# A new order for nearly all steps of a fused RWKV-7 and exact-GELU kernel

## The chip, the cores and the metric

The kernel runs on one core of one Trainium2 chip. The metric is the device time of one execution in microseconds (us); where a number of runs is given, it is their median. TensorE does the matrix products, VectorE and ScalarE the elementwise work, GpSimd fills constants and inverts small triangular blocks, and SyncE (SP) issues nearly all of the transfers. Each engine runs its own list of instructions in order, and waits on semaphores for the others.

## The reference

Two blocks follow each other. The first is the RWKV-7 recurrence over 768 steps for 4 batches and 8 heads of 40 columns; the second is a feed-forward block with the exact GELU. Cut to what is computed:

```python
# r, k, v, w, a, b: (4, 8, 768, 40) float32; state: (4, 8, 40, 40), zero at first
for t in range(S):
    y[:, :, t] = einsum('bhd,bhde->bhe', rt, state)
    Sa = einsum('bhde,bhe->bhd', state, at)
    state = state * wt[:, :, None, :] - einsum('bhd,bhe->bhde', Sa, bt)
    state = state + einsum('bhd,bhe->bhde', vt, kt)
x = y.transpose(0, 2, 1, 3).reshape(3072, 320)
h = x @ w_in                                    # w_in: 320 x 2048
g = 0.5 * h * (1.0 + erf(h * sqrt(0.5)))
return g @ w_out                                # w_out: 2048 x 320
```

`w_in` and `w_out` arrive as 64-bit floats. The kernel receives them as pairs of 32-bit words and makes 32-bit floats of them on the chip.

## The kernel before

**Chunks.** The sequence is cut into 12 chunks of 64 steps of time. Inside a chunk the recurrence is written as matrix products: cumulated decays, products of the scaled rows (`N`, `A`, `RV`, `QY`), the inverse of a unit triangular matrix of 64 x 64 for each head, and the state carried to the next chunk. The feed-forward block for the 256 rows of a chunk follows once its `y` is there. Chunks overlap: while the products of one chunk run, the inverse of the next one is under way and the feed-forward block of the one before fills TensorE.

**Steps.** Every piece of work is a *step*: a generator function whose name is a kind and a chunk, `N3` or `ph5`. Each time that a step is advanced, it emits the instructions up to its next `yield`. The kinds that matter here are these.

- `w`, `a`, `b`, `k`, `v`, `r` load a chunk's inputs (helper `load`, line 228, a DMA on SP's queue); `wi`, `wl` and `wo` load the words of the two weight matrices.
- `logs` (line 520) takes the logarithm of the decays in `w_tile`; `sums` forms their running sums on TensorE with the triangular mask `cum_m`; `sc` and `sk` scale the rows with them.
- `ta`, `tb`, `tk`, `tv`, `tr` are transposes on TensorE, through the helper `mm` of line 160, as most of the recurrence's products are.
- `N` is the product whose triangular part has to be inverted. It is written to memory by DMA. `nb` brings its 32 x 32 blocks back, with one block to a partition, to the tile `Nb`; `inv` inverts them on GpSimd, with 31 pairs of instructions for a chunk (lines 825 and 827), and stores the result. `corner` and `joined` bring it into place and multiply the blocks together. Chunk 0 has a way of its own, on TensorE: `sq`, `cornerd`, `joinedd`.
- `A`, `RV`, `av`, `X`, `sa`, `tn`, `yy`, `qk`, `QY`, `y` and `state` finish the chunk's recurrence.
- `ph` is the first feed-forward product, in a plain form for chunks 0 to 2 (line 1197) and in a form with fewer multiplications after that (lines 1222 and 1229). `pc`, `pd` and `pg` combine its parts and apply GELU on ScalarE and VectorE (lines 1258 to 1274); `po` is the second product (lines 1300 and 1316) and stores the output.
- `ci` and `co` turn the words of `w_in` and `w_out` into floats. VectorE and ScalarE share that work (lines 473 to 494).
- `consts`, `zeros`, `pads`, `gaps` and `tails` fill constant parts of tiles, nearly all on GpSimd; `consts` makes `cum_m` (line 353), `zeros2` clears columns of `VR`.
- `warm` and `begin` issue matmuls whose results nobody reads. `begin6` first has VectorE set a part of `w_in_sb` to 1 (line 1394), and then issues six of them.

TensorE takes its results in four tiles `duo0` to `duo3`, of two banks of PSUM each. A step that needs one takes the tile whose number stands behind its token.

**The order.** No scheduler orders the steps. A text of 1,554 tokens, `ORDER`, names at each place which step is advanced next, and after a colon which `duo` tile (and for conversions, which scratch tile) it takes:

```python
    ctx.enter_context(tc.manual_schedule(engines={mybir.EngineType.PE, mybir.EngineType.SP,
                                                 mybir.EngineType.DVE, mybir.EngineType.Pool,
                                                 mybir.EngineType.Activation}))
    going = {}
    for token in ORDER.split():
        queue[0] = nc.scalar if token[0] == "*" else nc.sync
        name, *at = token.strip("*").split(":")
        places[:] = [int(x) for x in at]
        if name not in going:
            kind = name.rstrip("0123456789")
            going[name] = steps[kind](int(name[len(kind):]))
        next(going[name], None)
```

So the list of instructions of each of the five engines, SP's transfers among them, is what this text lays down. A *pass* below is one weight load and one matmul as the hardware runs them; a product in 32-bit floats with one `matmul` call takes two passes. TensorE has 14,128 passes in an execution.

Of the kernel before, what the change touches and what calls it, by code (L numbers as in the profile page):

```python
# [34 lines left out]
sq1:1 sq1 placed0 av0:3 cornerd0 av0 tr1:0 ci9 wl0 shifts0 v1 tk1:2 cornerd0:1 wi0 ci4:1 placed2 zeros2 w2 tv1:3 cornerd0 consts0 joinedd0:1  # L35
r2 tr1 warm5:0 tv1 wo0 logs2 joinedd0 placed1 ci2:2 ci5 inv1 ci2 inv1 placed3 joinedd0 ci2 av0:3 av0 wi0 sums2:0 wi0 sa0:1
sa0 ci4 tk1 sa0:3 sums2:2 sa0 co1:0 a2 QY0:1:3 ci4 qk0 state0 sums2 y0 ta2:2 A1:1 tn1:3 co0:2 sums2 ci3:1 nb1 wi1
ci3 wi1 A1 co1 zeros8 r2 RV1:0 b2 co0 ta2 zeros6 wq3 tn1 y0:1 ci3 RV1 tr2:3 wi1 sc2 y0:2 tr2 y0
y0 inv1 yy1:3 yy1 av1:0:2 yy1 inv1 wi1 k2 co0 ci6:1 zeros5 ci7:2 tb2:1 inv3 wi1 co1 tb2 ci6 wo2 v2 ph0:3
ph0 sk2 ci7 inv1 ci6 zeros7 N2:1 ph0 X1 N2 ph0:1 wi1 ph0 co3:0 co3 ft1 ci7 X1 ci8:1 corner1:2 corner1:3 wo4  # L40
ci8 ph0 tk2:0 ft1 tv2:1 inv2 ft1 a3 co3 co2:2 a3 corner1 X1 co4:0 joined1:3 tk2 N2 A2:2 co2 ci8 co4 tv2
co2 joined1 ph0:0 A2 ph0 N2 ta3 wo6 ph0 joined1 co4 nb2 wo15 co7:1 co6:2 sa1:1:2 sa1 co6 co5:0 co7 wq3 w3
co6 bp3 RV2:3 ph0:0 sa1 ph0 wt3:2 QY1:1:2 w3 qk1 co7 RV2 co5 co5 tables1 wo9 bp3 po0:3 y1 po0 po0 state1
inv2 wt3 tn2:1 inv2 wo10 ph0 co11:1 k3 nb2 y1 y1 av2:0:2 logs3 wo8 tn2 vp3 y1 yy2:1 co11 kp3 wt3 kp3
y1 co11 inv2 po0 vp3 yy2 wt3 yy2 wo14 co8:0 co9:1 X2 tb3 co9 co8 ph1:1 ta3 tk3:2 X2 X2 ph1 sums3:0
sums3 co14:2 b3 co9 co14 r3 ph1 co8 wo13 co15:1 co10:0 N3:2 wo12 ph1:0 ph1 vp3 co15 co14 a4 co15 inv2 vp3
co13:2 N3 inv2 N3 co12:1 co10 N3 sc3 ft2 ph1 co12 co10 ft2 nb3 co13 r3 co12 ph1:1 ph1 tv3 A3:0 po1:2
nb3 co13 tails1 r3 po1 corner2:0 inv4 po0 po0 ft2 A3 corner2:0 po0 corner2 a4 ph1 po0 wq4 ta4 joined2:0 joined2 po0
r3 tr3 ph1:1 po0 joined2 sa2:3:0 wq4 wt4:1 sa2 ph1 wt4 bp4 sa2 QY2:3:0 wt4 qk2 ph1 bp4 sk3 po1 y2 state2
inv3 v3 vp4 RV3:1 RV3 po1 inv3 w4 w4 vp4 vp4 po0 vp4 tv4 wt4 y2 kp4 kp4 tn3:3 av3:0:1 tn3 yy3:3  # L50
tb4 yy3 y2 y2 po1 yy3 X3 a5 ta4 tk4:2 wq5 po0 N4:3 inv3 po1 N4 y2 po1 wq5 N4 wt5:0 ph2:3
X3 ws0 N4 inv3 inv3 ph2 wt5 ph2 ph2:0 ph2 ph2 r4 r4 ph2:3 ww0:1 ww0 nb4 nb4 inv4 wt5 ft3 logs4
ft3 inv4 ft3 corner3:2 ph2 ws1 ww0 ph2 corner3:0 corner3 po1 ws3 joined3:3 r4 a5 r4 po1 ph2:0 po1 vp5 vp5 ws2
# [24 lines left out]
kp9 ta9 kp9 yy8 wq10 po6 po6:2 wq10 po6 yy8 N9:3 po6 po6 po6 X8 X8 N9 po6:2 tk9:2 y7 N9 N9
po6 logs8 wt10:0 inv8 b8 tx7 tx7 po6 po6 po6:3 sums8:1 po6 inv10 wt10 nb9 tx7 nb9 wt10 X8 A9:2 A9 ft8
# [1363 lines left out]
```

## Time and profile before

| | before |
|---|---|
| median of 3 runs | 657.48 us (653.74 to 660.06) |
| profiled execution, its own time | 653.45 us |
| its span | 651.7 us |
| TensorE matmuls busy | 630.6 us, 97% |
| VectorE busy | 483.7 us, 74% |
| ScalarE busy | 273.5 us, 42% |
| GpSimd busy | 385.8 us, 59% |
| data moved by DMA | 80.78 MB, mean 124 GB/s |

The span runs from the first to the last instruction of the core; the execution's own time also holds what lies around it, 1.75 us here. TensorE's row is the one to read first: what it is not busy is all that an order of the same instructions can win back, unless the passes themselves run differently. In the tables of waits, the name behind the arrow is the instruction that ended an idle time; "issue" stands where the profile shows none.

### The profile page before, as it was taken

The numbers are of one execution on the slowest core, as the hardware profiler recorded it, in microseconds if no ns is written. First come the engines' busy times: TensorE is split into PE (matmuls) and PEld (weight loads), VectorE is DVE, ScalarE is ACT, GpSimd is POOL, SyncE is SP. The second block draws the span as 40 slices with busy tenths as digits, with TensorE's granted clock in tenths as the row PEclk, the third lists the DMA queues.
The fourth block names the chain that finished last, engine by engine and source line by source line (L and its number), as shares of the span: only waits on it lengthen the run. The fifth ranks groups of instructions, "written<-read, shape, count | busy, mean of one in ns | idle before, by whom it ended". The sixth has DMA issues, their size and how long they took to land.

```text
span 651.7 us, 31510 instructions
## 1 busy us (share of the span) xinstructions
PE 630.6 (97%) x14128; PEld 570.3 (88%) x14128; DVE 483.7 (74%) x643; ACT 273.5 (42%) x326; POOL 385.8 (59%) x797
## 2 busy tenths in 40 slices
PE   8998999999999999999999999999999899999997
PEld 4887778787888999999989988999999899999987
DVE  0797999996878997876967987886894884834442
ACT  2566465442434333524534345444433445135130
POOL 5058836845857866847857856868824877811000
PEclk9999999999999999999999999999999999999999
DMA  9989988679676867876786767697677866340100
GB/s 133 159 167 190 177 144 193 147 146 163 122 149 111 154 126 127 151 128 121 137 149 107 139 123 138 119 167 134 118 118 144 133 116 109 60 71 5 31 12 22
DMA packets 299112, 80.78 MB, mean 124 GB/s; under 512 B 287688, under 2 KB 292560, under 8 KB 298976
## 3 DMA queue, kind: packets, MB, share of 16 engines
q1 hardware_dynamic: 297872, 76.23, 65.1%
q0 software_dynamic: 864, 2.36, 2.2%
q8 instruction: 111, 1.82, 1.2%
q14 instruction: 25, 0.20, 0.1%
q10 hardware_dynamic: 240, 0.16, 0.1%
HBM read 65.40 MB, written 11.01 MB: 117 GB/s over the span
## 4 chain that ended last, share of the span: by engine, by line
PE 74%; DVE 7%; DMA 7%; SPq 6%; issue 3%; ACT 1%; POOL 1%; DVEq 0%; POOLq 0%; ACTq 0%
PE duo L160 22%; PE duo L1316 19%; PE duo L1222 15%; PE duo L1197 8%; SPq L228 6%; PE duo L1300 6%; PE duo L1229 4%; DMA inv<-rT 1%; DMA Tt<-inv 1%; DMA rows<-in_k_dram 1%; DMA rows<-N 1%; DMA rT<-in_k_dram 1%; DMA inv<-W 1%; DVE conv L493 1%; DMA rows<-in_b_dram 1%
## 5 line engine op out<-in xcount | busy, mean ns | idle before, releaser
L825 POOL TENSOR_TENSOR tmp<-W,Nb 128x56 f32<-128x56 f32 (+22 forms) x155 | 75.9, 490 | 56.6 <-DMA Nb<-N 45.0
L825 POOL TENSOR_TENSOR tmp<-rT,Nb 128x56 f32<-128x56 f32 (+22 forms) x155 | 78.6, 507 | 37.0 <-DMA Nb<-N 25.1
L1316 PE MATMUL duo<-w_out_sb,gt 128*128 128x160 f32 x640 | 93.2, 302 | 2.6 <-ACT gt L1274 1.2
L1316 PEld LDWEIGHTS duo<-w_out_sb,gt 128*128 128x128 f32 x640 | 87.7, 190 | 5.8 <-ACT gt L1274 1.4
L827 POOL TENSOR_TENSOR W<-W,tmp 128x56 f32<-128x56 f32 (+22 forms) x155 | 77.2, 498 | 12.2
L827 POOL TENSOR_TENSOR rT<-rT,tmp 128x56 f32<-128x56 f32 (+22 forms) x155 | 66.6, 430 | 12.1
L1222 PE MATMUL duo<-xt,w_in_sb 64*128 64x128 f32 x864 | 61.5, 275 | 0.0
L1266 DVE TENSOR_TENSOR gt<-gt,duo 128x1024 f32<-128x1024 f32 x27 | 32.7, 1213 | 34.6 <-ACT gt L1260 18.6
L1260 ACT COPY gt<-duo 128x1024 f32<-128x1024 f32 x27 | 27.3, 1012 | 73.7 <-PE duo L1222 46.3
L1229 PE MATMUL duo<-xt,w_in_sb 64*128 64x128 f32 x576 | 56.2, 272 | 0.0
L1197 PE MATMUL duo<-xt,w_in_sb 64*128 64x256 f32 x480 | 54.8, 381 | 1.0 <-DVE N L698 0.9
L1222 PEld LDWEIGHTS duo<-xt,w_in_sb 64*128 64x128 f32 x864 | 54.2, 188 | 1.7 <-DVE spare L698 0.5
L1197 PEld LDWEIGHTS duo<-xt,w_in_sb 64*128 64x128 f32 x480 | 45.5, 187 | 7.4 <-DVE N L698 1.2
L1316 PE MATMUL duo<-extra,conv 128*128 128x160 f32 x320 | 46.7, 302 | 1.2 <-issue 1.0
L1316 PEld LDWEIGHTS duo<-extra,conv 128*128 128x128 f32 x320 | 44.0, 190 | 2.3 <-issue 1.3
L1229 PEld LDWEIGHTS duo<-xt,w_in_sb 64*128 64x128 f32 x576 | 44.1, 188 | 0.0
L1272 ACT ACTIVATE gt<-gt 128x1024 f32<-128x1024 f32 x27 | 28.3, 1057 | 31.3 <-DVE gt L1266 31.3
L627 POOL TENSOR_TENSOR rows<-rows,w_tile 128x640 f32<-128x640 f32 x9 | 15.3, 1699 | 39.6 <-ACT w_tile L543 26.2
L1300 PE MATMUL duo<-w_out_sb,gt 128*128 128x320 f32 x128 | 36.9, 440 | 0.0
L1300 PEld LDWEIGHTS duo<-w_out_sb,gt 128*128 128x128 f32 x128 | 23.6, 190 | 9.4
L1320 DVE TENSOR_TENSOR os<-os,duo 128x160 f32<-128x160 f32 x40 | 12.7, 318 | 25.2 <-PE duo L1316 22.4
L968 ACT COPY SM<-duo 128x832 f32<-128x832 f32 (+1 forms) x22 | 17.4, 829 | 24.6 <-PE duo L160 24.6
(257 smaller groups left out, 1415.4 us busy)
## 6 DMA issues: line engine op xcount, KB each, us to landing
Nb<-N SPq DMA_DIRECT2D x18, 256.0 KB
VR<-in_v_dram SPq DMA_DIRECT2D x24, 160.0 KB
out_dram<-os SPq DMA_DIRECT2D x45, 80.0 KB
rows<-in_b_dram SPq DMA_DIRECT2D x22, 160.0 KB
rows<-in_k_dram SPq DMA_DIRECT2D x22, 160.0 KB
w_out_sb<-in_moe_w_out_dram SPq DMA_DIRECT2D x5, 640.0 KB
w_tile<-in_w_dram SPq DMA_DIRECT2D x36, 80.0 KB
Tt<-inv SPq DMA_DIRECT2D x44, 64.0 KB
```

Source lines behind the costliest of these rows:

```text
L160: nc.tensor.matmul(o, lhsT, rhs, start=first, stop=True, skip_group_check=True)
L228: queue[0].dma_start(out=out, in_=in_)
L825: eng.tensor_tensor(t, W[:, :nr, j:j + 1].to_broadcast([P, nr, rest]), Nb[:, j:j + 1, j + 1:].to_broadcast([P, nr, rest]), ALU.mult)
L827: eng.tensor_tensor(W[:, :nr, j + 1:], W[:, :nr, j + 1:], t, ALU.add)
L1197: nc.tensor.matmul(pt[:, x, s], w_in_sb[half(x), kt, p * P:(p + 1) * P], xt[half(x), kt], start=kt == 0, stop=kt == NK - 1)
L1222: nc.tensor.matmul(out_of(pt)[:, x, j], left(kt, j)[half(x)], right[half(x), kt], start=first and j == 0 and kt == 0, stop=True, skip_grou ...
L1229: nc.tensor.matmul(out_of(pt)[:, x, j], w_in_sb[half(x), NP, at:at + P], xt[half(x), NP, cols], start=False, stop=True, skip_group_check=True)
L1260: nc.scalar.copy(block_of(f, g), out_of(of(c)["u"]))
L1266: nc.vector.tensor_tensor(block_of(f, g), block_of(f, g), out_of(of(c)[v_]), ALU.add)
L1272: nc.scalar.activation(block_of(f, g), block_of(f, g), ACT.Gelu)
L1300: nc.tensor.matmul(pt[:, g], gt[:, f, g * P:(g + 1) * P], w_out_sb[:, f], start=f == 0, stop=f == NF - 1)
L1316: nc.tensor.matmul(pt[:, n, :DM // 2], l_[:, f], r_[:, f], start=f == 0, stop=f == NF // 2 - 1)
```

## The change

Only the text `ORDER` is new. It holds the same 1,554 steps (each step is advanced as many times as before), so every product, conversion and transfer is still made once, and no function changes. 76 advances stand at their old place. The others move by 12 places in the mean and by 6 in the median, most of all the first advance of `inv9` (207 places ahead) and the second of `tables0` (306 places back, a load of an activation table). Of the 328 tokens that name a tile, 261 now name another one. The tokens that the prediction speaks of, in a cut of the diff (the first six lines of the text):

```diff
-consts0 r0 begin6 wi0 pads1 gaps0 w0 logs0 zeros1 tails0 warm2:0 consts0 warm6:1 b0 inv1 begin6:2 sums0:3 pads2 w1 logs1 pads0 sums0:0
-sums1:1 sums0 a0 ta0:2 sums1:0 sums0 sc0 sums1 ta0 tb0:3 tb0 b1 warm0:0 zeros4 sc1 N0:2 N0 N0 warm1:0 pads3 v0 sq0
-a1 wl1 zeros3 tv0:3 tv0 wi0 sq0 sq1 sums1 sq0:0 sq1 sq0 sq0 sq1:2 tb1:3 ci0:0 sq0:1 ta1:0 r0 sq1 wi0 sq0
-sq1 sq0 tb1 ci0 wl1 ta1 sq1:2 wi0 ci1:1 sq0 sq1 sq1 k0 sq0:3 sq0 sq0 N1:1 N1 k1 sq1 sq1:0 r1
-sq0 sq1 gaps1 sk0 sq1 sq1 sq0:2 tables0 ci0 ci9:2 tk0:3 sq1:1 wi1 tr0:0 tk0 sq1 wi1 ci5:0 tr0 sq0 N1 ci1
-warm3:3 N1 r1 A0:3 sq1 sq0 RV0:0 zeros0 A0 RV0 sk1 wi0 sq0 sq1 tables0 ci1 nb1 sq0:2 ci5 sq0 wl0 ci9
...
+zeros1 w0 begin6 gaps1 logs0 tails0 begin6:0 a0 gaps0 consts0 warm2:1 zeros2 sums0:2 w1 b0 logs1 sums0:3 sums0 sums1:0 pads0 r0 sums0
+sc0 v0 ta0:1 warm0:3 sums1:2 tb0:3 sums1 tb0 b1 tables0 wi0 ta0 a1 consts0 wi0 N0:1 tv0:2 N0 sq0 warm3:3 sums1 sq0
+sc1 tv0 wi0 wi0 sq1 zeros4 sq1 sq0:0 sq0 sq0 N0 warm1:3 sq1:2 pads2 sq1 r1 ta1:3 sq0:0 sq0 pads1 ta1 tb1:1
+sq1 sq0 k0 tb1 sq1:2 sq1 sq1 r0 r1 sq0 zeros0 N1:3 N1 k1 sq0:1 sq1 sq0 sq1:0 sq0 N1 sk0 tk0:2
+zeros3 sq1 sq0 w2 N1 v1 tr0:3 wl1 ci1:0 ci1 sq1 sq0:1 sq1 ci1 sq1:0 tk0 A0:2 nb1 ci0:1 sq1 sq1 sq0
+tr0 sq0 sq0 warm6:3 sq1 tr1:3 sq0:1 ci0 sq0 sk1 logs2 sq1:0 wi1 RV0:1 wl0 sq1 wl0 pads3 ci0 wi1 tv1:0 tr1
...
```

`zeros2` stood at place 148 and stands at place 11 now, `warm6` went from 12 to 113, and the first advance of `inv1` from 14 to 154. `w0` was the seventh token and is the second. Most tokens of `co`, between places 182 and 419, stand 10 to 45 places nearer to the front; those of `ci` have moved both ways. For the rest the text keeps the same course, chunk by chunk, with neighbouring tokens exchanged.

More of the change, by code (lines that the diff above doesn't have):

```diff
@@ L34 @@
-warm3:3 N1 r1 A0:3 sq1 sq0 RV0:0 zeros0 A0 RV0 sk1 wi0 sq0 sq1 tables0 ci1 nb1 sq0:2 ci5 sq0 wl0 ci9
[L35 to L53, printed above, removed]
@@ new lines @@
+zeros3 sq1 sq0 w2 N1 v1 tr0:3 wl1 ci1:0 ci1 sq1 sq0:1 sq1 ci1 sq1:0 tk0 A0:2 nb1 ci0:1 sq1 sq1 sq0
+tr0 sq0 sq0 warm6:3 sq1 tr1:3 sq0:1 ci0 sq0 sk1 logs2 sq1:0 wi1 RV0:1 wl0 sq1 wl0 pads3 ci0 wi1 tv1:0 tr1
+warm5:3 wl1 RV0 cornerd0 wi0 consts0 cornerd0:1 placed2 A0 av0:3 placed0 wi1 wo0 wi0 cornerd0 wi1 av0 ci4:2 joinedd0:2 ci5:0 av0:1 ci9:1
+inv1 ci5 wi1 joinedd0 joinedd0 shifts0 tk1:3 placed3 wi0 nb1 placed1 av0 a2 ci5 wi1 sa0:2 ci9 r2 ci9 tv1 sa0 sa0:1
+tk1 sums2:0 ci2:0 ci2 sums2:3 co0:1 ci4 sums2 r2 sa0 wi0 QY0:2:1 ci2 b2 ci4 co0 inv1 qk0 k2 y0 state0 co0
@@ new lines @@
+v2 RV1:3 wo2 sums2 RV1 y0:2 ci6:0 ci3:2 ci7:1 ta2:1 A1:0 ci3 tr2:3 inv1 ta2 a3 tr2 zeros8 ci3 y0:1 tn1:3 wo6
+sc2 ci6 A1 inv1 inv1 y0 y0 sk2 zeros5 tb2:1 inv1 ci6 tn1 wi1 co3:2 av1:3:0 tb2 yy1:2 wi1 ph0:1 co1:0 yy1
+ft1 yy1 N2:2 ph0 co3 co1 co1 X1 wo4 ci7 co3 zeros7 N2 ph0 co7:0 co2:2 N2 ft1 co7 ci7 ft1 tv2:2
+X1 tv2 co2 ph0:1 N2 co7 tk2:3 corner1:1 co2 co6:0 corner1:2 a3 ci8:1 tails1 corner1 wo9 ph0 co5:2 ci8 tk2 co6 ci8
+nb2 co6 joined1:2 joined1 ph0 ph0:3 joined1 X1 ta3 ph0 co4:1 co4 w3 co5 sa1:1:0 RV2:2 ph0 wq3 co4 co5 wo10 sa1
```

103 lines of the change are left out of this document (57 added, 46 removed).

## The prediction

> **What bounds the kernel now.** I read the page from the top: shares of the engines, then who TensorE waits for, then the span in stages, then TensorE's own timeline where a wait has no releaser.
>
> ```profile
> span 651.7 us, 31510 instructions
> PE 630.6 (97%) x14128; PEld 570.3 (88%) x14128; DVE 483.7 (74%) x643; ACT 273.5 (42%) x326; POOL 385.8 (59%) x797
> PEclk9999999999999999999999999999999999999999
> q8 instruction: 111, 1.82, 1.2%
> ```
>
> TensorE is busy 97% of the span at a full granted clock in every slice. The order of the steps changes no matmul, so a new order can only win or lose in what is not work: 651.7 - 630.6 = 21.1 us of idle time, and in what the passes lose against each other. The last row is a queue that carries instructions alone: 1.82 MB in 111 packets is 16.4 KB a packet, and TensorE has 2 x 14128 = 28256 instructions (a weight load and a matmul for each pass), 255 to a packet. So one packet feeds about 128 passes, the number in the change's description.
>
> ```profile
> PE duo L160 <- issue: 5.0, 7, 1.2
> PE duo L160 <- POOL cum_m L353: 2.2, 1, 2.2
> PE duo L160 <- POOL rows L825: 1.4, 1, 1.4
> ...
> PE duo L1316 <- ACT gt L1274: 1.2, 1, 1.2
> PE duo L1316 <- issue: 1.0, 2, 0.7
> ...
> PE duo L1222 <- issue: 0.8, 1, 0.8
> ```
>
> These are TensorE's waits (total, times, longest). Ten of them, 5.0 + 1.0 + 0.8 = 6.8 us, wait for nothing that the profile shows. 2.2 us is the start, 1.4 us a wait for GpSimd; the other 10.7 us of the 21.1 are many waits for VectorE and ScalarE of at most 1.2 us, and gaps too short for the view. Two neighbours among the ten, in TensorE's timeline (start, length, row, idle before):
>
> ```profile
> 318.57 1.70 PE L160 MATMUL duo<-VR,nT 64*64 64x104 f32 x64
> 320.03 1.18 PE L160 MATMUL duo<-rT,turned 40*64 40x64 f32 x64
> 321.14 1.08 PE L1316 MATMUL duo<-extra,conv 128*128 128x160 f32 x6
> 322.97 3.69 PE L1316 MATMUL duo<-extra,conv 128*128 128x160 f32 x26 [0.75 <-issue]
> 326.59 1.16 PE L160 MATMUL duo<-aT,nT 40*64 40x64 f32 x64
> 327.57 1.07 PE L160 MATMUL duo<-st,aT 40*64 40x104 f32 x38
> 329.37 0.83 PE L160 MATMUL duo<-st,aT 40*64 40x104 f32 x25 [0.72 <-issue]
> ```
>
> Both stalls cut through a run of equal matmuls, and between them lie 26 + 64 + 38 = 128 passes. TensorE has run out of instructions there: the next packet of 128 passes is late. The ten stalls sit on this grid of 128 passes. The stalled piece behind 322.97 took 5.4 us of work, the one ahead of it 58 + 64 + 6 passes from about 318.7, some 3.4 us. Short pieces are at risk, with no sharp threshold.
>
> ```profile
> 32.00:65.00 33.00, 30.22 (x872) 26.61 (x866) 29.19 (x49) 20.97 (x29) 23.10 (x45) 1.00 0.89 177
> 65.00:98.00 33.00, 30.21 (x777) 25.20 (x773) 30.71 (x53) 17.03 (x24) 19.38 (x43) 1.00 0.93 160
> 98.00:130.00 32.00, 30.90 (x636) 25.53 (x630) 29.88 (x46) 16.94 (x22) 23.69 (x49) 1.00 0.77 171
> 130.00:163.00 33.00, 32.97 (x492) 25.79 (x492) 26.35 (x45) 11.28 (x16) 16.47 (x41) 1.00 0.88 154
> ```
>
> The stages (TensorE, weight loads, VectorE, ScalarE, GpSimd, clock, DMA share): from 32 to 130 us VectorE is as full as TensorE (30.71 and 30.21 of 33 us), because the f64 weights are converted there. From 130 us on TensorE alone is full.
>
> **The change, part by part.** Every step is still issued once; engines, sizes, transfers and dummy matmuls are the same. What moves is each engine's queue.
>
> *Instruction supply.* I cut TensorE's list of instructions, before and after, at the grid of the stalls and priced each piece from start to start:
>
> ```profile
> 342.05 1.95 PE L1222 MATMUL duo<-rT,rows 64*128 64x128 f32 x32
> 343.83 1.95 PE L1222 MATMUL duo<-xt,conv 64*128 64x128 f32 x32
> ...
> 348.39 0.75 PE L160 MATMUL duo<-conv,N 32*32 32x32 f32 x64
> 349.08 1.16 PE L160 MATMUL duo<-aT,kT 40*64 40x64 f32 x64
> 350.17 0.75 PE L160 MATMUL duo<-Tt,Js 32*32 32x32 f32 x64
> ...
> 357.88 0.39 PE L1229 MATMUL duo<-xt,w_in_sb 64*128 64x128 f32 x4
> 358.20 1.66 PE L160 MATMUL duo<-SM,rows 64*64 64x104 f32 x64
> 359.67 1.52 PE L160 MATMUL duo<-VR,rows 64*64 64x104 f32 x60
> ```
>
> 64 passes of 32x32 take 0.69 us, of 64x64 1.09, of 64x104 1.47, 32 of 64x128 1.78; the 26 passes of 128x160 above take 3.62. So 128 passes last from 1.4 to 18 us, by what is in them. Before, 3 pieces are under 3 us (2.3, 2.5, 2.8) and 19 under 4; after, 7 (1.8, 2.1, 2.5, 2.6, 2.6, 2.7, 2.8) and 23. Against 4.5 us, about the middle of the two stalled pieces above (3.4 and 5.4), the short pieces lack 24 us in all before and 35 after. On the chip's grid, then, the new order spreads the long passes no better, but somewhat worse. At 6.8 us of stall for 24 us lacking, 35 give 9.9: +3.1. Looked at with the 32 passes ahead of each piece, which a queue would cover, the eight shortest fall from a mean of 4.3 to 4.0 us: 8 x 0.3 = +2.4. I take +2.7; the bounds are -6.8 (no stall left) and +8.8 (all 23 pieces under 4 us stall, at the mean of the ten, 0.68 us: 15.6).
>
> The Trainium skill says otherwise in "Runtime: NRT & Kernel Launch", section "Instruction fetch mechanics": the sequencer fetches the next 16 KiB while it executes this one, and crossing the boundary is mostly hidden. This case's trace has ten crossings that are not, 6.8 us; by the page this term would be 0 and the sum 2.7 us lower.
>
> *Changes of shape.* After the four 64x128 passes at 357.88, 0.22 us of work by the rate above, the next start is 0.32 us later: about 0.1 us for a change of shape. There are 518 changes before and 531 after: 13 x 0.1 = +1.3, between 0 and +2.
>
> *The start.*
>
> ```profile
> 0.82 1.45 SPq L228 DMA_DIRECT2D r_pairs<-in_r_dram  x2
> ...
> 1.00 0.48 DVE L1394 MEMSET w_in_sb<- 128x512 f32 x1 [1.00 <-PEq L1427]
> 2.17 3.78 PE L160 MATMUL duo<-cum_m,ident 128*128 128x512 f32 x4 [2.17 <-POOL cum_m L353]
> ...
> 2.99 1.31 SPq L228 DMA_DIRECT2D w_tile<-in_w_dram  x2
> ...
> 5.74 6.05 PE L160 MATMUL duo<-w_in_sb 128*128 128x512 f32 x12
> ...
> 9.92 0.74 ACT L520 ACTIVATE w_tile<-w_tile 128x640 f32<-128x640 f32 x1
> ...
> 11.72 1.16 PE L160 MATMUL duo<-cum_m,w_tile 64*64 64x64 f32 x64
> ```
>
> TensorE's dummy passes now begin with `begin6`, which needs VectorE's memset (done at 1.48) and not GpSimd's mask (2.17), and one pair (`warm6`, 0.86 us) leaves the front. So the first real passes can start 0.7 + 0.86 = 1.5 us sooner, if the logarithm is ready: `w0` goes first on SP's queue instead of third, 2.2 us sooner, which brings its end from 10.66 to about 8.5. `warm6` stands later, in the stage from 32 us where TensorE idles 2.8 us, so it may cost up to 0.86 there. I take -1.0 (0 to -1.5).
>
> *Waits for other engines.* `zeros2` (a memset of `VR`) moves on GpSimd's queue from behind the inverse `inv1` to near the front, so the wait of 1.4 us for GpSimd goes; VectorE sets part of that stage, so I count half: -0.7. For the others I set each TensorE instruction's distance (in TensorE work) from the one that releases it against the delay that this producer's line usually has in the trace: 47 of some 330 are closer than the delay before, 38 after. That is a fifth fewer tight places on about 6.5 us (10.7 less the gaps below the view, some 4 us): -1.3, between -4 and +4, since few tight places became waits. The round trip from the product `N` by DMA, GpSimd and DMA to `corner` keeps 51 to 69 us of TensorE work as cover (53 to 66 before), so I cost the moved DMA issues and SP's queue at 0; without that cover GpSimd's chain would lie bare, some 30.6 us for each inverse (five of the ten are in these two rows: 75.9 + 77.2 us):
>
> ```profile
> L825 POOL TENSOR_TENSOR tmp<-W,Nb 128x56 f32<-128x56 f32 (+22 forms) x155 | 75.9, 490 | 56.6 <-DMA Nb<-N 45.0
> ...
> L827 POOL TENSOR_TENSOR W<-W,tmp 128x56 f32<-128x56 f32 (+22 forms) x155 | 77.2, 498 | 12.2
> ```
>
> The sum: +2.7 + 1.3 - 1.0 - 0.7 - 1.3 = +1.0 us. The profiled execution took 653.45 us (1.75 around its span), the median of the runs is 657.48, 4.0 above it. So 654.5 for an execution like the profiled one, and 658.5 for the median.
>
> **The rivals.** (1) *Faster, the waits go.* The stalls for instructions vanish (-6.8) with the other terms as above (-1.7): 657.5 - 8.5 = 649. For it speaks that the plan has fewer tight places and a long piece ahead of a short one can cover it (pieces of 2.3 and 2.5 us passed without a stall); against it, the count of short pieces.
>
> (2) *Slower, VectorE becomes the bound between 80 and 130 us.* The weight conversions (`co` above all) stand earlier in VectorE's queue. Summed over the queue with each line's mean from the trace, VectorE must do 76.6 us of work ahead of TensorE's pass 2,200 before, and 85.1 after: 8.5 us more in front of the same pass, and other results that TensorE waits for queue behind it. In the trace this pass starts at 104.3, and VectorE has idled some 10 us by then (6.1 of it in the two stages from 32 to 98). If it idles as much again, the pass comes 8.5 - 1.5 = 7 us later, and TensorE, full from 130 us on, never makes it up: 657.5 + 7 = 664.5, and with the supply term 667. It decides from the point where VectorE's idle time can't shrink by 7 of those 10 us. Against it: at pass 2,970, where the last converted weights are used, VectorE's work is equal (126.1 and 126.4), so the lead is given back before the stage ends.
>
> (3) *Slower, more stalls*: the upper bound, +8.8, less 1.7 of the others: 664.6.
>
> (4) *The grid hides all*: crossings cost nothing more than now, so the supply term is 0: 655.8. It is the page's rule above, and the ten stalls speak against it.
>
> **How the numbers follow.** The forecast, small terms of both signs, has a chance of 0.50, rival 1 0.18, rival 2 0.14, rival 3 0.10, rival 4 0.08. One per cent, about what a measurement of this kernel can tell from no change, is 6.6 us: faster below 650.9, slower above 664.1. Forecast and rival 4 lie within: 0.58; faster 0.18; slower 0.24. Predicted is the likeliest, 658.5. Its own range is 653 to 664 (terms at their near bounds); to leave out no more than 2 in 10 it must reach into rivals 1, 2 and 3: 648 to 669.
>
> **What would show it.** Right: TensorE waits "<- issue" of 7 to 12 us in ten to sixteen places 128 passes apart, most behind the pieces under 3 us; the first 64x64 passes near 10.3 us; no wait for GpSimd at the `VR` transposes; VectorE still near 30 of 33 us from 65 to 130 us. Wrong: fewer than 4 us of "<- issue" (rival 1, and my grid is no measure), or the pass 2,200 after 108 us with VectorE waits on TensorE ahead of it (rival 2), or a wait for a DMA in the inverse's round trip, which I cost at nothing.

## The result, and the profile after

The changed kernel is slower: 674.54 us (674.33 to 675.71, four runs) against 657.62 us in the same session, a ratio of 1.0267 with a 95% interval of 1.0215 to 1.0318. The forecast was 658.5 us, in a range of 648 to 669. The profiled execution took 674.72 us, its span 673.0 us, 21.3 more than before. In all that follows medians and ratios are of fast runs, that is without an execution more than 1.5% above the fastest of its kernel.

The page of the changed kernel, its first lines and TensorE's clock in 40 slices:

```profile
span 673.0 us, 31524 instructions
PE 643.4 (96%) x14128; PEld 577.8 (86%) x14128; DVE 482.3 (72%) x643; ACT 273.7 (41%) x326; POOL 377.6 (56%) x797
PEclk9998899999999999899799999999999999999999
```

The passes are the same 14,128, yet TensorE is busy 12.8 us longer (643.4 against 630.6) and idle 8.5 us longer (29.6 against 21.1). The third row says why much of the same work took longer: before, the granted clock was full in every slice, and now it dips in three places.

TensorE's waits (total, times, longest):

```profile
PE duo L160 <- issue: 7.4, 6, 4.2
PE duo L160 <- DVE rT L583: 4.7, 2, 2.6
PE duo L1316 <- issue: 2.0, 2, 1.2
PE duo L160 <- DVE w_in_sb L1394: 1.5, 1, 1.5
PE duo L160 <- DVE gt L1266: 1.3, 1, 1.3
PE duo L1316 <- ACT gt L1274: 1.2, 1, 1.2
...
PE duo L160 <- POOL rows L825: 1.1, 1, 1.1
```

Waits for instructions come to 9.4 us, 2.6 more than before, but one of them alone is 4.2 us. A row that before did not have is second: 4.7 us behind `DVE rT L583`, the transposition of `r` in two later chunks.

I then looked at each dip of the clock, in windows cut where the clock changes (busy time and count of TensorE, weight loads, VectorE, ScalarE, GpSimd; clock, DMA share, GB/s):

```profile
54.10:57.50 3.40, 0.40 (x25) 0.39 (x26) 0.00 (x0) 0.00 (x0) 2.85 (x8) 1.00 1.07 245
57.51:60.92 3.41, 3.41 (x52) 3.10 (x46) 2.25 (x3) 1.81 (x3) 2.94 (x7) 0.50 1.03 213
...
71.16:74.57 3.41, 1.82 (x92) 1.55 (x82) 3.38 (x6) 0.00 (x0) 3.02 (x6) 1.00 0.88 147
74.58:77.99 3.41, 2.82 (x14) 1.90 (x16) 3.38 (x8) 1.03 (x1) 2.78 (x9) 0.50 0.90 238
272.55:275.96 3.41, 1.33 (x94) 1.24 (x95) 2.50 (x3) 3.38 (x4) 2.94 (x7) 1.00 0.91 159
275.97:279.37 3.40, 3.40 (x70) 2.43 (x59) 3.37 (x5) 2.54 (x4) 3.09 (x5) 0.50 1.35 163
323.75:327.15 3.40, 0.85 (x40) 0.65 (x32) 1.21 (x2) 3.35 (x4) 2.93 (x7) 1.00 0.43 69
327.17:333.98 6.81, 6.74 (x82) 6.62 (x83) 6.67 (x11) 1.06 (x1) 5.87 (x13) 0.50 0.81 121
```

The rows go in pairs. In a window of 3.4 us TensorE is busy for 0.40, 1.82, 1.33 and 0.85 us, and in the next window the clock is at 0.50 (in the last pair for two windows). These windows come to 17.1 us. At half clock they cost up to 8.5 us, so most of the 12.8 us of longer work; where the other 4.3 us of it come from stays open. Such a wait is paid a second time, after it is over. The Trainium skill describes this in "TensorE: Matmul & The Clock Gate", section "Part 1: The HAM clock gate (the "warmup" mystery)": a free-running window of 3,413 ns, and half clock after an idle one. The lengths agree; but the window need not be idle throughout, since here 1.82 busy us of 3.41 did not keep the clock. Nor is there one sharp limit in the traces of this case: in before a window with 2.00 busy us (from 48.18 us) kept it, in graft_w one with 1.57 (from 296.80), and in shift64 one with 2.39 (from 45.90) lost it.

Where the time is lost I read from the starts of passes, since both kernels work through the stages in one sequence. In the columns is the time between two passes (us), from the trace of one execution of each kernel. The last column ends with the start of the last pass. The kernels below the line are the experiments, described further down.

| kernel | 855 to 1,660 | 1,660 to 5,000 | 5,000 to 7,600 | 7,600 to end |
|---|---|---|---|---|
| before | 33.1 | 164.3 | 108.2 | 295.3 |
| after | 40.5 | 165.3 | 116.9 | 297.8 |
| | | | | |
| h3_before_then_r_early | 34.3 | 166.6 | 108.1 | 302.2 |
| r_early | 41.3 | 166.4 | 107.8 | 296.9 |
| r_late | 34.8 | 166.3 | 112.0 | 293.8 |
| warm_fill | 41.6 | 165.4 | 113.1 | 299.6 |
| wi_early | 41.6 | 166.8 | 108.4 | 295.3 |
| loads_spread | 36.6 | 166.4 | 115.2 | 298.9 |
| graft_w | 31.4 | 189.1 | 112.5 | 298.3 |

After loses 7.4 us between passes 855 and 1,660 (48 to 89 us in its span) and 8.7 between 5,000 and 7,600 (254 to 371 us): 16.1 of the 21.3.

One execution each is a rough measure of a stage. Where the order of before is unchanged in the first of these stages, its time lies between 31.7 us (h1) and 37.6 (copies_calm); where that of after is unchanged, between 38.2 (h4) and 41.6 (warm_fill). In the second, kernels that have the order of after there lie between 112.2 us (loads_later) and 117.8 (wo0_late), those with that of before between 106.9 (h4) and 109.9 (copies_50). So the two losses stand clear of this spread, but a difference of 4 us between two rows can be chance.

The first of these places in TensorE's timeline of after (start, length, row, idle before):

```profile
52.21 0.69 PE L160 MATMUL duo<-w_in_sb,Nb 32*32 32x32 f32 x31
...
57.10 0.82 PE L160 MATMUL duo<-w_in_sb,Nb 32*32 32x32 f32 x33 [4.21 <-issue]
...
57.85 3.04 PE L160 MATMUL duo<-VR,nT 64*64 64x104 f32 x32
```

A run of equal passes is cut in two, on the grid of packets, as in the stalls of before; the 32 passes behind it take 3.04 us at half clock where their like took 1.64 at 50.64 us. By the trace's record of the instruction queue this packet began to move at 54.5 us and had landed at 55.5; TensorE went on 1.6 us later. When it was asked for is not recorded. I count from the time at which TensorE began the 128 passes ahead of it, 49.5 us: by this estimate it stood 5.0 us in line. All times in line below are such estimates. The stall is no chance of one run: in the profiles of after and of h2, h4, r_early, warm_fill, wo0_late, loads_later and loads_later_r_early below it is 2.6 to 5.5 us.

The second place in the timeline of all engines:

```profile
262.43 2.79 SPq L228 DMA_DIRECT2D w_tile<-in_w_dram  x4
265.31 1.52 SPq L228 DMA_DIRECT2D out_dram<-os  x2
266.88 1.09 SPq L228 DMA_DIRECT2D v_pairs<-in_v_dram  x2
268.07 0.93 SPq L228 DMA_DIRECT2D a_pairs<-in_b_dram  x2
269.04 2.67 SPq L228 DMA_DIRECT2D r_pairs<-in_r_dram  x4
...
273.42 1.25 DVE L583 STREAM_TRANSPOSE rT<-r_pairs 128x1024 f32<-128x1024 f32 x1 [2.19 <-DMA r_pairs<-in_r_dram]
...
274.72 1.16 PE L160 MATMUL duo<-rT,late 40*64 40x64 f32 x64 [2.08 <-DVE rT L583]
```

SP issues without a pause, and the last four loads of `r` for chunk 5 stand behind 10 others. VectorE waits 2.19 us for them, TensorE 2.08 us for VectorE.

### The profile page after: what moved, and what is told of

It is laid out like the page before. It is cut to its first block, busy times and chain, and to the rows that moved or that the text cites. A ratio compares the mean times of both kernels' runs of the same rounds, so it can differ in the third digit from the quotient of the medians.

```text
span 673.0 us, 31524 instructions
## 1 busy us (share of the span) xinstructions
PE 643.4 (96%) x14128; PEld 577.8 (86%) x14128; DVE 482.3 (72%) x643; ACT 273.7 (41%) x326; POOL 377.6 (56%) x797
## 3 DMA queue, kind: packets, MB, share of 16 engines
q8 instruction: 111, 1.82, 1.2%
## 4 chain that ended last, share of the span: by engine, by line
PE 69%; DMA 9%; DVE 8%; SPq 5%; POOL 5%; issue 3%; ACT 2%; DVEq 0%; ACTq 0%; POOLq 0%
PE duo L160 21%; PE duo L1316 20%; PE duo L1222 15%; PE duo L1197 5%; SPq L228 5%; PE duo L1229 4%; PE duo L1300 3%; POOL tmp L825 3%; POOL W L827 2%; DMA w_out_sb<-in_moe_w_out_dram 2%; DMA a_pairs<-in_a_dram 2%; DMA a_pairs<-in_b_dram 1%; PE duo L578 1%; DVE gt L1266 1%; DMA r_pairs<-in_r_dram 1%
## 5 line engine op out<-in xcount | busy, mean ns | idle before, releaser
L825 POOL TENSOR_TENSOR tmp<-W,Nb 128x56 f32<-128x56 f32 (+22 forms) x155 | 75.2, 485 | 76.3 <-DMA Nb<-N 64.5
L1316 PE MATMUL duo<-w_out_sb,gt 128*128 128x160 f32 x640 | 96.1, 309 | 1.2 <-ACT gt L1274 1.2
L825 POOL TENSOR_TENSOR tmp<-rT,Nb 128x56 f32<-128x56 f32 (+22 forms) x155 | 70.2, 453 | 46.4 <-DMA Nb<-N 34.6
L1316 PEld LDWEIGHTS duo<-w_out_sb,gt 128*128 128x128 f32 x640 | 90.7, 195 | 4.3 <-ACT gt L1274 1.4
L827 POOL TENSOR_TENSOR W<-W,tmp 128x56 f32<-128x56 f32 (+22 forms) x155 | 75.1, 484 | 12.1
L827 POOL TENSOR_TENSOR rT<-rT,tmp 128x56 f32<-128x56 f32 (+22 forms) x155 | 71.2, 459 | 12.1
L1222 PE MATMUL duo<-xt,w_in_sb 64*128 64x128 f32 x864 | 62.8, 276 | 0.0
L1229 PE MATMUL duo<-xt,w_in_sb 64*128 64x128 f32 x576 | 57.0, 272 | 0.2 <-DMA xt<-last 0.2
L1197 PE MATMUL duo<-xt,w_in_sb 64*128 64x256 f32 x480 | 56.6, 383 | 0.2 <-ACT nT L642 0.2
L1300 PEld LDWEIGHTS duo<-w_out_sb,gt 128*128 128x128 f32 x128 | 23.6, 190 | 9.7 <-issue 0.3
L993 DVE TENSOR_TENSOR SM<-duo,left_upper 128x832 f32<-128x832 f32 (+1 forms) x22 | 21.0, 990 | 9.1 <-PE duo L160 9.1
```

The lines of the kernel that those rows point to most:

```text
L825: eng.tensor_tensor(t, W[:, :nr, j:j + 1].to_broadcast([P, nr, rest]), Nb[:, j:j + 1, j + 1:].to_broadcast([P, nr, rest]), ALU.mult)
L827: eng.tensor_tensor(W[:, :nr, j + 1:], W[:, :nr, j + 1:], t, ALU.add)
L1197: nc.tensor.matmul(pt[:, x, s], w_in_sb[half(x), kt, p * P:(p + 1) * P], xt[half(x), kt], start=kt == 0, stop=kt == NK - 1)
L1222: nc.tensor.matmul(out_of(pt)[:, x, j], left(kt, j)[half(x)], right[half(x), kt], start=first and j == 0 and kt == 0, stop=True, skip_grou ...
L1229: nc.tensor.matmul(out_of(pt)[:, x, j], w_in_sb[half(x), NP, at:at + P], xt[half(x), NP, cols], start=False, stop=True, skip_group_check=True)
L1300: nc.tensor.matmul(pt[:, g], gt[:, f, g * P:(g + 1) * P], w_out_sb[:, f], start=f == 0, stop=f == NF - 1)
```

## The experiments

The theory: half of the loss is a late packet of instructions between 50 and 60 us, held up by a bunch of loads of `w_in`; the other half is two late loads of `r`; and each wait is followed by half clock. The main rival: no place is special, and the new order has many more small waits everywhere.

**Where the loss lies.** Two kernels join the orders at a cut.

```diff
 h1: tokens 1 to 275 of before, then all others in the order of after
 h2: tokens 1 to 255 of after, then all others in the order of before
```

> The first 275 tokens in the order of before, the other 1279 in the order of after; the cut lies at pass 1,972, about 95 us. Theory (three places: a late packet of instructions and half clock at 50 to 83 us, two late loads of r and half clock at 272 to 334 us): by pass 2,040 the changed kernel had lost 12.7 of the 21.3 us between the two profiles, so this kernel keeps 8.6 of 21.3, or 6.8 of the 16.9 us between the medians: 664.5 us (662 to 667), with full clock until 270 us and the waits for L583 still there. Rival (many small waits, spread evenly over the passes): the prefix holds 14% of the passes, so 14% of the loss goes: 672 us.

> The reverse: the first 255 tokens in the order of after, the rest in the order of before; the cut lies at pass 2,076, about 107 us. Theory: it keeps the 10.4 to 12.7 us lost ahead of 107 us and nothing else: 668 us (666 to 670), half clock near 58 and 75 us, full clock later. Rival (spread evenly): 657.6 + 0.15 x 16.9 = 660 us.

In h2 the product `av` of chunk 1 is overwritten in PSUM before it is copied; the work and the transfers are the same. It took 664.86 us (ratio 1.0129, 1.0079 to 1.0179), 7.5 above before: less than the theory's 668, well above the rival's 660. h1 took 673.75 us (1.0243, 1.0204 to 1.0282), which neither theory expected at that cut. Its waits on TensorE show why:

```profile
PE duo L160 <- ACT Js L940: 7.3, 1, 7.3
```

The seam itself made a wait of 7.3 us at 102 us and 6.8 us of half clock behind it, so h1's total says nothing. Two better cuts followed.

```diff
 h3: tokens 1 to 620 of before, then after, with r_early (below); scratch tiles renumbered behind the cut
 h4: tokens 1 to 322 of after, then before
```

> The first 620 tokens in the order of before (pass 4,804, about 236 us), the rest in the order of after, with the loads of r for chunks 5 and 6 brought forward as in r_early. Theory: the loss of after lies ahead of 107 us and at these two loads; this kernel has neither: 658 to 660 us, with at most one stretch of half clock before 640 us. Rival (the rest of the order carries a loss of its own): the profiles differ by 9.1 us behind pass 4,800, and 5.0 + 5.1 of that are the r loads; if something else takes their place, 664 us or more.

> The first 322 tokens in the order of after, the rest in that of before; the cut lies at pass 2,436, about 126 us. Theory: the loss of the first part stands alone: h2, cut at 107 us, was 7.5 us above before, and h3 against r_early gave 10.0 for the first 620 tokens; so 657 + 8.5 = 665.5 us (663 to 668). Rival (the first part's loss is caught up, since the passes behind it are waiting for other things): 660 us or less.

h3 took 660.08 us against 656.77 (1.0058, 1.0025 to 1.0091) and h4 663.92 against 656.12 (1.0123, 1.0081 to 1.0166): 7.8 us for the first 322 tokens alone, as the theory says. h3 lies at the upper end of what its theory gave, and keeps 3.3 us by the medians (1.6 to 6.0 by the interval) that neither place explains.

**The loads of r.**

```diff
 r_early, on after (chunk 5; chunk 6 alike)
-r5 ph3 r5 A5:2 ... pg3 bp6 tx3 r5 qk4 ph3 state4 logs5 pg3 pd3 r5 tr5
+r5 ph3 r5 r5 r5 A5:2 ... pg3 bp6 tx3 qk4 ph3 state4 logs5 pg3 pd3 tr5
 r_late, on before
-... vp6 pg3 r5 bp6 ph3 pc3 sa4 r5 sa4 pd3 QY4:3:1 qk4 state4 tr5 ph3 pg3 w5
+... vp6 pg3 bp6 ph3 pc3 sa4 sa4 pd3 QY4:3:1 qk4 state4 w5 r5 r5 tr5 ph3 pg3
```

> The order of after with the second half of the loads of r for chunks 5 and 6 (two tokens each) right behind their first half, 25 and 13 to 16 tokens nearer to the front. No engine but SP gets another order. Theory: the two waits for L583 (2.2 + 2.8 us) go, and with them the half clock at 276 and 327 to 334 us (10.2 us at half speed, worth 5.1): 674.5 - 10.1 = 664.5 us (663 to 667). Rival 1 (the half clock there has another cause than the wait): 669.5 us. Rival 2 (another load is late next, since SP issues as many transfers as before): 672 us or more.

> The order of before with only the second half of the loads of r for chunks 5 and 6 (and one load of w5 ahead of it) moved back, to right ahead of the transposes that read them. Theory: TensorE waits 2 to 4 us twice behind DVE rT L583, and each wait brings one or two stretches of half clock of 3.4 us (worth 1.7 each): 657.3 + 5 + 4 = 666 us (662 to 669). Rival (a late r hides behind other work, as the prediction costed it): 657 us.

r_early took 670.49 us (1.0196, 1.0151 to 1.0241), 4.0 less than after; the theory wanted 10. In its profile the theory holds in full at the place itself: passes 5,000 to 7,600 take 107.8 us, as in before, and the waits behind L583 and the half clock are gone:

```profile
270.00:280.00 10.00, 10.00 (x248) 9.39 (x249) 8.88 (x12) 9.56 (x10) 8.74 (x16) 1.00 0.82 144
...
320.00:330.00 10.00, 9.69 (x245) 9.19 (x241) 8.37 (x13) 6.09 (x6) 8.77 (x16) 1.00 0.75 133
330.00:340.00 10.00, 9.91 (x315) 9.43 (x318) 9.40 (x9) 2.29 (x6) 9.06 (x13) 1.00 0.79 162
```

That execution took 666.82 us, the other three 669.1 to 672.2; they left no trace, so where they lost part of it again is not known. r_late took 659.93 us (1.0051, 1.0029 to 1.0073), 3.2 more than before, where the theory wanted 9. Only chunk 6's load came late: a wait of 2.1 us behind L583, two more behind it, and one stretch of half clock, together the 3.8 us of its row in the table. (A second stretch, at 70.4 us, stands where its order is still that of before: before, too, loses the clock in some executions.) Chunk 5's did not; the direction is shown, the size was taken too large.

**The clock.**

```diff
 warm_fill, on after (dummy matmuls whose results nobody reads)
-... ph3 RV5:2 ... state5 RV6:1
+... ph3 warm10:2 warm11:2 RV5:2 ... state5 warm12:1 warm13:1 warm14:1 RV6:1
```

> The order of after, with dummy matmuls of warm (128x512, nobody reads them) put ahead of the products RV5 and RV6 that wait for r: two and three of them, 1.7 and 2.6 us of work, into the two waits for L583. The waits stay as long. Theory (the clock halves because TensorE idles through most of one 3.4 us window): the half clock at 276 and 327 to 334 us (10.2 us, worth 5.1) goes: 669.5 us (668 to 672). Rival (it halves for another cause, such as light passes or power): 674.5 us, or 1 more for the dummies.

It took 674.52 us (1.0289, 1.0219 to 1.0358): no gain, as the rival said. But the clock did what the theory says, in the stretch that was at 0.66, 0.72 and 0.60 in after:

```profile
275.00:280.00 5.00, 3.88 (x141) 2.32 (x139) 3.68 (x5) 3.62 (x4) 4.30 (x10) 1.00 1.01 156
...
325.00:330.00 5.00, 5.00 (x130) 3.15 (x125) 2.98 (x5) 3.91 (x4) 4.26 (x10) 1.00 0.63 108
330.00:335.00 5.00, 5.00 (x76) 4.76 (x71) 4.93 (x7) 1.07 (x1) 4.37 (x9) 1.00 0.77 109
```

Passes 5,000 to 7,600 took 113.1 us in place of 116.9, dummies included, which is within the spread of kernels without dummies. This one profile does not settle it alone, since without dummies waits behind L583 of 1.74 us (loads_later), 2.03 and 1.88 us (graft_w) left the clock full too. What speaks for the theory is all traces together, cut every 3.413 us from the first change of the clock on: half clock begins only behind windows of 3.4 us in which TensorE was busy 2.4 us or less, and each window with less than 1.5 us is followed by it. That mostly idle windows halve the clock is shown by this; that keeping TensorE busy pays here is not (its runs: 671.9 to 679.8).

**The bunch of w_in loads.** Three edits on after take loads out of it, with one, then five, then nine loads moved:

```diff
 wo0_late:     wo0 moved back by 24 tokens
 loads_later:  wo0 and four of wi1 moved back, by 18 to 29 tokens
 loads_spread: loads_later, and two of wl1 and two of wi1 brought forward, by 25 to 63 tokens
```

> The order of after with one transfer moved: wo0 (640 KB of w_out's words) 24 tokens later, behind the bunch of w_in loads that SP issues between 40 and 51 us. Theory: the packet of instructions asked for at 49.5 us stood 5.0 us behind these loads; at some 200 GB/s 640 KB are 3.2 us, so the stall of 4.2 us at 52.9 us shrinks to about 1.5 and the half clock behind it (3.4 us, worth 1.7) goes: 674.5 - 2.7 - 1.7 = 670 us (668 to 672). Rival (the stall comes from the short piece alone, 3.4 us of work, whatever the load queue holds): 674.5 us.

> The order of after with five transfers of the weights' words moved back: four of w_in (256 KB each) that are first read 60 tokens later, and wo0 (640 KB). It takes 1.7 MB out of the bunch that SP issues between 41 and 51 us, and no engine but SP gets another order. Theory: the packet of instructions asked for near 50 us then waits 2 to 3 us in the transfer queues, as elsewhere, not 5.0; the stall of 4.2 us behind it shrinks to 1 to 2, and the half clock near 57 us goes with it (1.7 to 3.4): 674.5 - 2.7 - 2.5 = 669.3 us (667 to 671). Rival (as in wo0_late, other transfers move up and the queue stays as full): 674 us.

> Both edits of transfers on the order of after: loads_later and r_early. Theory: they add up, 674.5 - 5.2 - 4.0 = 665.3 us (663 to 668). Rival (loads_later does nothing): 670.5 us, as r_early alone.

> The order of after with the bunch taken apart to both sides: the five transfers of loads_later moved back, and four more (two of wl1, two of wi1) brought forward by 25 to 63 tokens, to about where the order of before has them. Theory: the packet near 50 us waits 2 to 3 us, the stall of 4.2 us falls to 1 to 2 and the half clock at 57 us goes: 668.5 us (666 to 671). Rival (the late packet has another cause in this order): 673 to 675 us, with a packet wait over 4 us.

wo0_late (673.79 us; 1.0243, 1.0208 to 1.0278) and loads_later (673.06 us; 1.0256, 1.0199 to 1.0314) did nothing clear of noise, as their rival said: the packet near 50 us stood 6.2 and 4.5 us in line. In wo0_late the loads behind moved up: SP issued ten of `w_in` from 40.62 to 48.64 us. loads_spread took 670.62 us (1.0195, 1.0132 to 1.0258). TensorE's timeline at the same passes:

```profile
52.77 0.69 PE L160 MATMUL duo<-w_in_sb,Nb 32*32 32x32 f32 x32
53.73 0.69 PE L160 MATMUL duo<-w_in_sb,Nb 32*32 32x32 f32 x32 [0.27 <-issue]
```

The packet stood 0.8 us in line, the stall fell from 4.21 to 0.27 us, and no half clock follows. So these loads, where after has them, held the packet up; this rests on one profile, against eight with the stall. The stage gains 3.9 of the 7.4 us; another wait of 2.0 us (for `SM`, L983) brings its own half clock at 64 us. Loads of `r` early and five loads later together, loads_later_r_early, took 667.36 us (1.0173, 1.0135 to 1.0212), in the range of its theory, but not by its way: the stall at the same passes was still 4.42 us, so what it gains over r_early (3.1 us) is not explained.

The reverse test, on before:

```diff
 wi_early, on before
-tables0 ci1 nb1 sq0:2 ci5 sq0 wl0 ci9 ... wi1 ... wi1 ... wi1 ... wi1
+tables0 ci1 nb1 sq0:2 wi1 wi1 wi1 wi1 ci5 sq0 wl0 ci9
```

> The order of before with four loads of w_in's words (256 KB each, in 4 KB packets to their own places) brought forward by 70 to 100 tokens to pass 782, where the order of after has its bunch; nothing else moves. Theory (this bunch fills the transfer queues, and a packet of instructions stands in line): the packet asked for near 52 us waits 4.5 to 6 us in place of 3.0, the stall behind it is 3 to 4 us, and half clock follows: 656 + 5 = 661 us (659 to 665). Rival (copies_50 put 1.3 MB there and the packets waited 2.4 to 3.6 us: instructions are not held up by such loads, data is): packet waits as in before, and 655 to 658 us.

665.81 us (1.0127, 1.0064 to 1.0189), 8.7 more than before, for four loads out of 1,554 tokens. But the way is another than expected:

```profile
50.00:55.00 5.00, 1.17 (x12) 1.20 (x14) 1.40 (x4) 1.14 (x2) 4.20 (x11) 0.78 0.91 155
55.00:60.00 5.00, 5.00 (x89) 4.40 (x86) 3.08 (x5) 2.32 (x3) 4.37 (x9) 0.50 1.01 257
60.00:65.00 5.00, 4.60 (x94) 3.16 (x93) 2.67 (x4) 3.12 (x5) 2.19 (x6) 0.70 0.95 134
```

The packet near 47 us stood 3.4 us in line and did no harm, the next one 3.7 us with a stall of 0.4; TensorE waited 4.95 us at the transposes of `VR`, and 10.2 us of half clock followed. The view puts this wait down to `POOL rows L825`, but by the semaphores that these transposes wait for it ended with the second load of `v` for chunk 1: its last piece landed at 53.59 us, and TensorE went on at 53.84. Two kernels with copies of `w_in` in 4 KB packets, put into before, say the same:

```diff
 copies_50, copies_calm: five such copies near 45 us; six near 380 us
+        t = dram.tile([HP, wd], UINT32, tag=f"junk{c}", name=f"junk{c}")
+        load(t, words_from(32 * c, [(4 * wd, HP)], 0, 0))
```

> The order of before with five such copies near pass 782, 45 us, where the profile of after has its bunch of w_in loads. Theory: the packet asked for near 52 us waits 5 us or more (3.0 in before), the stall behind it grows from 1.4 to 3 to 4 us and brings one or two stretches of half clock, worth 1.7 each; the inputs behind the copies come later too: 656.6 + 6 = 662.5 us (660 to 667), which would show the first part's loss in the order of before. Rival (the stall in after comes from its short piece, not from the queue): the packet waits 3 us and the time is 656.6 to 658 us.

> The order of before with six more transfers in a calm stage (near pass 8,300, 380 us, where the queues are busy 0.7 of the time): 256 KB of w_in's words each, copied in 4 KB packets to a place in memory that nobody reads. 384 packets at 226 to 324 ns on 16 engines are 5.4 to 7.8 us of all queues. Theory (a packet of instructions stands in line with the loads): the one or two asked for in that time wait 3 to 6 us in place of the 1.1 that is the median there, and TensorE stalls 2 to 4 us once or twice more, perhaps with one stretch of half clock: 656.6 + 4 = 660.5 us (659 to 664). Rival (instructions go ahead of data): packet waits of 1 to 2 us and 656.6 us.

copies_50 took 661.79 us (1.0105, 1.0057 to 1.0154), with a wait of 5.8 us for `DMA VR<-in_v_dram` at the place where wi_early waits; copies_calm 658.82 us (1.0052, 1.0013 to 1.0091), with 3.7 us behind L932, in the inverse's round trip. The packets of instructions stood at most 3.6 and 3.0 us in line near the copies, not 5. copies_calm also shows chance at work: at 59 us, long before its copies, a packet stood 4.6 us in line and TensorE waited 2.8 us, in the very order in which before's profile has a stall of 1.2. Too many loads at once cost the stage some 8 us in wi_early and copies_50; whether data or instructions come late depends on what stands where in the queues, and what decides that stays open.

```diff
 graft_w, on after: the 103 tokens of wi, wl, wo, ci, co where before has them, counted in TensorE passes
 graft_w_r_early: the same with r_early
```

> The order of after, with all loads and conversions of the weights (wi, wl, wo, ci, co; 103 tokens) put where the order of before has them, counted in TensorE passes; three conversions and the memset of their constant stand a few tokens earlier, as what reads them needs. Between 42 and 57 us the profile of after moves 2.3 MB in 4 KB packets of these words, at 324 ns each, that of before 1.1 MB at 226 ns. Theory (these loads fill the transfer queues when a packet of instructions is asked for): the packet near 50 us waits some 3 us as in before, the stall of 4.2 us falls to 1 to 2 and the half clock behind it goes; of the 7.5 to 8 us that the first part costs (h2, h4) most is won: 667.5 us (665 to 670). Rival (the stall and the waits of that part come from TensorE's own order there, a piece of 3.4 us): 674 us (672 to 676).

> graft_w and r_early together. Theory: 667.5 - 4 to 7 = 662 us (660 to 665), what is left being the 3.8 us of h3 and a little of the first part. Rival (graft_w does nothing): 670 us.

695.52 and 692.86 us (1.0580 and 1.0542): a miss. Passes 855 to 1,660 take 31.4 us, even less than in before, but graft_w waits 6.08 us behind `ACT w_in_sb L895` ahead of them (up to 49.38 us, pass 694), so this says little. Conversions and the products that read them no longer meet (4.9 us behind `DVE w_out_sb L494`), and the next stage takes 189.1 us. The loads' place is part of an order that hangs together.

**The grid.** The prediction's first term, measured by itself:

```diff
 shift64, on before; after_shift64, on after
+        for n in range(32):
+            mm(pt[:32, 1, :32], w_in_sb[:32, 0, :32], w_in_sb[:32, 0, :32])
```

> The order of before, with 64 small dummy passes (32x32, 0.7 us) behind begin6: nothing moves but the grid of 128 passes by which TensorE's instructions arrive, by half a packet. Theory of the prediction's first term: on the shifted grid the short pieces lack about 45 us against 4.5 us each (24 before, 35 after), and stalls grow in proportion, from 6.8 to some 12.7 us: 657.3 + 5.9 + 0.5 = 663.5 us. Rival (the stalls depend on what the transfer queues hold, not on the count of short pieces): within 2 us of 657.5.

> The order of after with the 64 small dummy passes of shift64 behind begin6. Theory: both orders stand at the best place of the grid for themselves, before more so: with each kernel's pieces and packet waits of 0.7 to 2.1 us I work out 14.7 us of stalls for before and 29.2 for it shifted (measured in the profiles: 9.5 and 22.3), 20.1 for after and 26.2 for it shifted. So shifting costs after 5 to 6 us of stalls and some half clock, 3 to 6: 683 us (679 to 687), much less than the 22 of before. Rival (after's order is made so that each packet has long passes, wherever the grid lies): 675 us.

shift64 took 677.11 us (1.0319, 1.0251 to 1.0388): 64 dummy passes that last 0.7 us made the kernel slower by 20.3 us, more than the whole change did. Its waits:

```profile
PE duo L160 <- issue: 17.0, 13, 3.1
...
PE duo L1229 <- issue: 1.2, 1, 1.2
...
PE duo L1316 <- issue: 0.8, 1, 0.8
```

19.0 us for instructions where before had 6.8, and 24 us at half clock behind them; its waits for other engines did not grow. after_shift64's runs lie from 671.6 to 687.8 us (1.0317, 1.0232 to 1.0403), too far apart for a size. In its profile, of the run of 687.8 us, waits for instructions come to 13.8 us against 9.4, so they grow by 4.4 us, not by 12.2 as in shift64. That before fits its grid more closely than after would agree with this; one execution does not show it.

**The sum.** By medians, after is at 674.54; with the loads of `r` early 670.49 (4.0 us); with the first 620 tokens in the order of before as well 660.08 (10.4 us, most of it the stage of the `w_in` loads); before is at 656.77 in that session (3.3 us in the rest of the order, whose place stays open). Half clock is a share of each: by the mean clocks of the runs, I estimate that after spends some 16 us at half clock in a run, before some 4; at half speed that is 6 of the 17 us. No kernel tried beats before.

## Why the prediction was wrong, by its own steps

- *Instruction supply, +2.7.* The size came out, by luck: 9.4 us of "issue" against 6.8, +2.6. But in eight places, not ten to sixteen, and with 4.2 us in a single one. What it lacks in short pieces did not make that stall; the time that the packet stood in line did, 5.0 us where the median of the packets from 30 to 130 us is some 1.4. And the rule of proportion (stalls as what the short pieces lack) gave +5.9 for the shifted grid, where +12.2 was measured.
- *Changes of shape, +1.3.* No run tests it alone. With the mean spacing that each pair of sizes has in before's trace (passes behind an idle time left out), I estimate 629.1 us for the passes of after against 628.0: +1.1, too little to matter.
- *The start, -1.0.* The first 64x64 passes begin at 10.10 us, 1.6 earlier. It is given back, first at 18.91 us, where the passes of `N0` wait 1.10 us for ScalarE: by 26.7 us before has started 342 passes and after 337.

```profile
10.10 1.16 PE L160 MATMUL duo<-cum_m,w_tile 64*64 64x64 f32 x64
...
18.91 1.16 PE L160 MATMUL duo<-aT,nT 40*64 40x64 f32 x64 [1.10 <-ACT nT L642]
```

- *The wait for GpSimd, -0.7.* The wait at the `VR` transposes is gone, but it never was one for GpSimd. In before `zeros2` did not stand behind the inverse's rows, which begin at 46.74 us: its memset of `VR` was over at 38.81 us, 10 us before the wait began (in the order of time, from the timelines of GpSimd, SP and TensorE).

```profile
38.23 0.58 POOL L391 MEMSET VR<- 128x384 f32 x1
...
43.33 1.85 SPq L228 DMA_DIRECT2D VR<-in_v_dram  x2
...
50.30 1.97 PE L160 MATMUL duo<-ident,VR 128*64 128x128 f32 x32 [1.42 <-POOL rows L825]
```

  What ended it was the second load of `v` for chunk 1, whose last piece landed at 50.16 us by the semaphore's record. In after SP issues these loads at 37.28 us, 6 us earlier. The term had the right sign by luck; its cause was the place of a load in SP's queue, which the prediction cost at 0. The row `POOL rows L825` of after, 1.1 us at 75.17 us, is another wait, ended by VectorE (L1120, done at 75.02).
- *Other waits, -1.3 (between -4 and +4).* This is the step that failed. I priced each wait by TensorE's distance to the instruction that releases it, with that line's usual delay, and "the moved DMA issues and SP's queue at 0". A transposition whose input is late has no usual delay: `r5`'s last load stood six tokens ahead of `tr5` before, and one ahead now. L583 alone brought 4.7 us, and TensorE's waits for other engines together grew from 10.0 to 16.1 us, by 6.1 where the two terms gave -2.0.
- *The clock.* It was not in the sum at all. The clock of before was full in every slice of its profile, and I took that as given; in the traces here it falls behind windows of 3.4 us in which TensorE was busy 2.4 us or less, if not behind all of them. In after's profile 17.1 us went at half clock, up to 8.5 us on top of the waits of 2.1 to 4.2 us.

The rivals fared no better. VectorE did not become the bound (rival 2): it is nearly full from 65 to 98 us (32.72 of 33 us), and pass 2,200 comes at 113.0 us instead of 104.3, which was one of its signs. But no wait for VectorE longer than 0.2 us stands between 84 and 107 us, and pass 1,660 is already 9.0 us late (89.0 against 80.0): the 8.7 us come from the stage ahead, not from VectorE's queue. Rival 3 had the right side and 664.6 us, from stalls alone. Rival 4, that crossings are hidden (in the Trainium skill's "Runtime: NRT & Kernel Launch", section "Instruction fetch mechanics"), is refuted by shift64: 15 crossings were not, 19.0 us.

## What to carry to other kernels

When only an order changes, look at the transfer queue with the same care as at the engine that bounds: ask of each load how many transfers stand ahead of it and when its reader needs it. A wait of some 2 us or more on TensorE may be paid twice, once for itself and once for the window of half clock behind it; whether it is depends on how it falls into the windows (2.08 us in after were, 2.03 us in graft_w were not). And where a view names an engine as what ended a wait, look whether that engine's result was ready long before: the wait may be for a load. And when a long list of instructions runs with little slack, an edit at its front shifts the grid of all later packets, so compare orders on the grid on which they will run.

## What was not expected of the hardware

A packet of instructions needs about 1.2 us to move and, at a stall, some 1.5 us from landing to the next pass; what varies is its time in line, by the estimate above 0.6 to 1.0 us in the median from 130 us on in before and after, and 4.5 to 6.2 us near 50 us in after, wo0_late, loads_later and r_early. The clock fell to half behind windows of 3.41 us in which TensorE was busy 0.40 to 1.82 us in after, and up to 2.39 us in shift64. Sixty-four passes of 32x32 put in at the front (0.7 us) cost 20 us at the end.
